# A fused attention and mixture kernel: loads written into the searched order, exponentials in place and in pairs, and a new order at the entry of the last stage

## The chip, the cores and the metric

One core of one Trainium2 chip runs the whole program. The metric is the device time of one execution in microseconds (us); lower is better. The engines are PE (TensorE; PEld are its weight loads), DVE (VectorE), ACT (ScalarE), POOL (GpSimd) and SP (SyncE, which here issues all the DMAs, strictly one after the other).

## What is computed

Three layers follow each other. Every number is float32 except w_in and w_out of the last layer, which arrive as float64 words and are turned into two narrower parts on the chip.

```python
# 1. attention with pooled keys and values: 8 batches, 8 heads, 576 queries, 72 keys of 64
k_p, v_p = k.mean over groups of 8, v.mean over groups of 8
s = q @ k_p.T / 8;  a = exp(s - max(s));  a = a / (sum(a) + 1e-9);  x = a @ v_p
# 2. soft mixture of 8 experts with 4 slots each, x is 4608 x 512
logits = x @ phi                        # 4608 x 32
d = softmax(logits over the rows);  slots = d.T @ x
out_e = relu(slots_e @ w1[e]) @ w2[e]   # w1: 512 x 1024, w2: 1024 x 512
x = softmax(logits over the slots) @ out
# 3. last layer
h = x @ w_in;  u = h * softmax(h);  ln = (u - mean(u)) / sqrt(var(u) + 1e-6) * g
y = ln @ w_out                          # 4608 x 512
```

## The kernel before

Attention works in 12 blocks n = 0..11 of 384 queries; three blocks belong to two batches b. Each block takes four pairs of heads (hp = 0..3). Its steps have short names, and one long string of names (`order`, about 730 steps) is the program order of all five engines in this stage: each engine runs its own steps in the order in which they stand there.

- On DVE: `K{b}.i` sums eight keys (L289), `M{n}.hp` takes the maxima of the scores (L371), `A{n}.hp` subtracts them into one of three spare buffers `dd_buf` (L376), `U{n}.hp` sums the exponentials (L393), `r` inverts the sums (L402), `q`, `l`, `m`, `g1`, `g2`, `gj` are small steps of the logits and the group maxima.
- On ACT: `k{b}.i` copies the summed keys (L294, L295), `E{n}.hp` takes the exponentials (L388 for hp 0, 2, 3; hp 1 is done as six short instructions straight from PSUM, L385), `t{n}.c` copies turned chunks (L419), `w`, `x`, `y` copy small products.
- On PE: `S{n}.hp` scores (L363; a float32 matmul shows as two records), `T{n}.c` transposes (L413), `P`, `X`, `Y` products of the values, `L{n}` logits (L429), `G{i}.n` the weighted sums of a group of blocks (L516).
- On POOL: `V{b}.0..2` sum eight values (L303 to L308), `R` a guard (L398), `N{n}.half` the normalisation of half a block in `a_rows` (L407). `ND` lists the halves that DVE takes in its place, here block 10, half 0.

All of attention's loads (`k0..k7`, `q0..q11`, `v0..v7`) and the first weights go through one ring buffer of 88 KB per partition: a load can be issued once the last reader of what lay there is done. They are written ahead of the order string; a planner of the framework chose where each stands in SP's queue. After them follow `D0` to `D6`: weights of the experts that are loaded into attention's own buffers when these come free (`early` holds the keys, the three spare buffers, the pooled keys and values; `a_rows` the exponentials; `late` the turned chunks). `D0` and `D1` hold the eight chunks of expert 7.

After attention, `first(e)` (L797, PE) multiplies the slots with w1 of the experts in the order 1, 2, 7, 4, 0, 5, 3, 6. Then a second hand-written list, `steps`, sets the order: `h0`, `h1` scale the hidden rows (ACT L950, DVE L952), `ph` turns them (PE L956), `B0` to `B15` multiply with w2 (PE L965), `ao2` begins the conversion of the third part of w_out (ACT L870), which is loaded into the place of `W_hi`. Behind `B15` come `a0`, `a1` (the rows of the slots copied by ACT and DVE into one tile `s2`, L1015), `s0..s3`, `so`, the conversion of the last part of w_in in halves (`aj bj sj tj +j`), `M0 M1 N0 N1` (PE L1034), `mh0 mh1` (ACT), `c0..c8` (column sums of w_out, PE L971/L972). Then the entry of the last stage: three tiles with `f` (PE L1102/L1105), `x`, `k`, `u`, `w` (DVE), `e`, `h`, `S` (ACT), `n`, `t`, `P` (PE), `T` (DVE L1162). From the seventh tile on a loop runs: per tile 24 matmuls with W_hi and W_lo (L1282, L1283, L1285), two for the next tile (L1192), and work of the other engines four tiles ahead.

Of the kernel before, what the change touches and what calls it, by code (L numbers as in the profile page):

```python
# [64 lines left out]
ND = ((10, 0),)  # L65
# [19 lines left out]
def moe_attention_kernel(ctx: ExitStack, tc, q, k, v, phi, w1, w2, w_in, w_out, g, out):  # L85
# [61 lines left out]

    for p in range(NP):
        b, n = 2 * p, NB * p
        kv_tile(kT, b, "kT")  # L150
        q_tile(n)
        if p == 0:
            for h in range(HP):
                load_kv(kT, k, b, h, h + 1)
                load_q(n, h, h + 1)
        else:
            load_kv(kT, k, b)
            load_q(n)
        for what in (LO0 if p == 0 else LO).split():
            if what == "k1":  # L160
                kv_tile(kT, b + 1, "kT")
                load_kv(kT, k, b + 1)
            elif what[0] == "v":
                kv_tile(vT, b + int(what[1]), "vT")
                load_kv(vT, v, b + int(what[1]))
            elif what == "phi":
# [66 lines left out]
    if True:  # L233
# [1212 lines left out]
```

## Time and profile before

| | us |
|---|---|
| median of three executions | 421.54 (421.21 to 423.11) |
| the profiled execution | 424.87 |
| its span, first to last instruction | 423.1 |
| PE busy in the span | 390.0 (92%) |
| DVE, ACT, POOL busy | 314.1, 295.1, 220.7 |
| read from HBM | 70.32 MB |

A "wait" in these profiles is the idle time of an engine ahead of an instruction, with what ended it in brackets. The clock column is the granted TensorE clock: 1.00 is 2.4 GHz, 0.50 is 1.2 GHz. "us to landing" of a DMA counts from its issue on SP to its completion.

### The profile page before, as it was taken

The page shows a single profiled execution, that of the slowest core. Times are in us where ns is not written, and L with a number is a line of the kernel's source. Part 1 is how long each engine was busy: PE and PEld are TensorE (multiplying, and loading weights), DVE is VectorE, ACT ScalarE, POOL GpSimd, SP SyncE. Part 2 cuts the span into 40 slices and gives each one's busy share as a digit, 9 for nine tenths or more (in the row PEclk, how much of TensorE's full clock was granted, in tenths as well). Part 3 has the DMA queues.
Part 4 walks back from the last instruction along what each step waited for, and adds up shares of the span by engine and source line. Part 5 has one row for each costly group of instructions (what it writes and reads, how often), then busy time and mean ns, then how long its engine had stood idle before and what let it go on. Part 6 is the DMA issues. An engine that isn't in the chain of part 4 may idle for free.

```text
span 423.1 us, 8679 instructions
## 1 busy us (share of the span) xinstructions
PE 390.0 (92%) x3204; PEld 235.3 (56%) x3204; DVE 314.1 (74%) x511; ACT 295.1 (70%) x663; POOL 220.7 (52%) x410
## 2 busy tenths in 40 slices
PE   4679899999989979878889989999999999999996
PEld 4568798988877435432345434444444444444445
DVE  3796999989834876894689977777777877878720
ACT  2578899899876646953469986667776666777631
POOL 4298589588540120000027687666666776666630
PEclk9996999999999997989899999999999999999999
DMA  8999999977979997994000388757666476695781
GB/s 271 389 395 417 391 419 397 362 255 270 335 277 370 400 425 310 417 419 162 0 2 1 93 167 189 161 94 169 139 135 161 89 173 156 97 174 128 141 180 50
DMA packets 86074, 97.10 MB, mean 230 GB/s; under 512 B 69904, under 2 KB 74768, under 8 KB 80144
## 3 DMA queue, kind: packets, MB, share of 16 engines
q1 hardware_dynamic: 86032, 96.55, 72.3%
q8 instruction: 25, 0.41, 0.4%
q14 instruction: 17, 0.14, 0.1%
HBM read 70.32 MB, written 9.44 MB: 189 GB/s over the span
## 4 chain that ended last, share of the span: by engine, by line
PE 52%; DMA 5%; DVE 3%; ACT 2%; issue 1%; SPq 0%; DVEq 0%; ACTq 0%
PE o L1282 14%; PE o L1283 14%; PE o L1285 13%; DMA w<-in_w_dram 4%; PE h L1192 3%; PE p L965 3%; PE pc L936 1%; DMA vhi<-v 1%; PE ph L956 1%; PE pu L1142 1%; DVE nm L1112 0%; PE o L1401 0%; PE o L1398 0%; PE h L1105 0%; PE o L1399 0%
## 5 line engine op out<-in xcount | busy, mean ns | idle before, releaser
L1282 PE MATMUL o<-W_hi,vhi 128*128 128x512 f16 x280 | 107.1, 382 | 1.6 <-DMA vhi<-v 1.6
L1283 PE MATMUL o<-W_lo,vhi 128*128 128x512 f16 x280 | 107.1, 383 | 0.0
L1285 PE MATMUL o<-W_hi,vlo 128*128 128x512 f16 x280 | 66.9, 380 | 0.0
L1204 ACT ACTIVATE e<-h,nm 128x1024 f32<-128x1024 f32 x33 | 36.7, 1113 | 43.0 <-DVE nm L1197 43.0
L363 PE MATMUL sc<-early,qT 128*128 128x144 f32 x320 | 54.4, 321 | 10.6 <-ACT early L295 9.2
L363 PEld LDWEIGHTS sc<-early,qT 128*128 128x128 f32 x320 | 47.7, 215 | 14.3 <-ACT early L295 6.0
L1263 DVE TENSOR_TENSOR v<-v,v 128x1024 f16<-128x1024 f32 x32 | 39.2, 1224 | 14.0 <-ACT v L1246 13.9
L1282 PEld LDWEIGHTS <-vhi 128*128 128x128 f16 x280 | 27.5, 98 | 35.6 <-DMA vhi<-v 2.1
L1283 PEld LDWEIGHTS <-vhi 128*128 128x128 f16 x280 | 27.6, 98 | 32.6 <-issue 0.8
L1197 DVE TENSOR_REDUCE nm<-h 128x1 f32<-128x1024 f32 x33 | 40.4, 1223 | 6.6 <-PE h L1192 6.5
L1210 DVE CUSTOM_DVE_ANT_0 u<-h,e 128x1024 f32<-128x1024 f32 x33 | 40.3, 1223 | 6.2 <-ACT e L1204 6.1
L407 POOL TENSOR_TENSOR a_rows<-a_rows,rs 128x864 f32<-128x864 f32 x23 | 37.5, 1635 | 12.1 <-DVE rs L402 4.8
L1285 PEld LDWEIGHTS <-vlo 128*128 128x128 f16 x280 | 25.1, 98 | 33.6 <-issue 7.8
L1246 ACT ACTIVATE v<-u,b,sr 128x1024 f32<-128x1024 f32 x33 | 40.8, 1236 | 1.5 <-POOL b L1234 1.5
L1221 ACT ACTIVATE e<-u,nmu 128x1024 f32<-128x1024 f32 x33 | 37.9, 1149 | 0.4 <-POOL nmu L1216 0.4
L371 DVE TENSOR_REDUCE nmax<-sc 128x6 f32<-128x432 f32 x48 | 28.3, 597 | 9.9 <-PE sc L363 9.7
L1259 DVE TENSOR_SCALAR v<-u,nmu,sr 128x1024 f16<-128x1024 f32 x32 | 26.0, 811 | 10.2 <-POOL sr L1232 10.2
L413 PE MATMUL pt<-ident,a_rows 128*128 128x128 f32 x180 | 28.3, 284 | 3.8 <-ACT late L419 2.3
L1228 POOL TENSOR_TENSOR y<-y 128x1 f32<-128x1 f32 x33 | 30.3, 918 | 2.7
L1232 POOL TENSOR_TENSOR sr<-z,exponents 128x3 f32<-128x3 f32 x33 | 29.2, 883 | 2.7
L419 ACT ACTIVATE late<-pt 128x384 f32<-128x384 f32 x60 | 27.7, 490 | 4.1 <-PE pt L413 3.4
L1295 ACT ACTIVATE ob<-o,r 128x512 f32<-128x512 f32 x32 | 21.7, 679 | 9.7 <-PE o L1285 9.7
(246 smaller groups left out, 741.0 us busy)
## 6 DMA issues: line engine op xcount, KB each, us to landing
w<-in_w_dram SPq DMA_DIRECT2D x16, 1024.0 KB, 10.9
vT<-in_v_dram SPq DMA_DIRECT2D x8, 1152.0 KB, 12.4
out_dram<-ob SPq DMA_DIRECT2D x11, 768.0 KB, 3.6
kT<-in_k_dram SPq DMA_DIRECT2D x7, 1152.0 KB, 12.0
w<-in_w_dram SPq DMA_DIRECT2D x12, 512.0 KB, 4.8
qT<-in_q_dram SPq DMA_DIRECT2D x7, 768.0 KB, 12.9
a_rows<-in_w_dram SPq DMA_DIRECT2D x4, 1024.0 KB, 9.0
qT<-in_q_dram SPq DMA_DIRECT2D x8, 384.0 KB, 10.9
```

Of the source, the lines that this page charges most:

```text
L363: pe.matmul(sc[:, r].rearrange("p h j -> p (h j)"), qT[n][:, hp, x, :], BD[b % NBD][:, hp, :], start=(i == 0), stop=(i == len(hv) - 1))
L407: eng.tensor_tensor(av, av, st["rs", n, hf].unsqueeze(3).to_broadcast([P, NR, 4, J]), ALU.mult)
L1197: dve.tensor_reduce(nm, ft[i][0], axis=AX.X, op=ALU.max, negate=True)
L1204: act.activation(e, hv, AF.Exp, bias=nm, accum_out=st[:, 0:1])
L1210: dve.tensor_tensor_reduce(u, hv, e, 1.0, 0.0, ALU.mult, ALU.add, st[:, 1:2])
L1221: act.activation(e, u, AF.Square, bias=nmu, accum_out=st[:, 2:3])
L1228: pool.tensor_tensor(y, y, y, ALU.mult)
L1246: act.activation(v, u, AF.Identity, bias=b, scale=sr[:, 0:1])
L1263: dve.tensor_tensor(v2, u_t[i]["v"], u_t[i]["v1"], ALU.subtract)
L1282: pe.matmul(po, hi[:, c, :], W_hi[:, c, :], start=(c == 0), stop=False)
L1283: pe.matmul(po, hi[:, c, :], W_lo[:, c, :], start=False, stop=False)
L1285: pe.matmul(po, lo[:, c, :], W_hi[:, c, :], start=False, stop=(c == NFC - 1))
```

## The change

1. The loads of attention after the first pair of batches, and the first weights, are steps of the order string now (`ik3`, `iq4`, `iv2`, `ia1.2`, `io0`, `ir4`, `ib0.1`): SP issues them in the written order. Keys go ahead of queries; w_out's first two parts (`io0`, `io1`), which stood between `q5` and `v3`, go far back.
2. `A` writes into the place of the exponentials in `a_rows`, `E` works in place, and heads 2 and 3 of a block are one instruction of `E` and of `U`. The three spare buffers fall away, and three of expert 7's eight chunks (`ir7`) are loaded into their place in the midst of attention; `D1` shrinks from four chunks to one.
3. Sixteen matmuls of the identity with itself (`F0` to `F15`) are added to PE's queue; their result is not used.
4. DVE no longer takes a normalisation (`ND` is empty).
5. The order of attention is a new one.
6. `s2` becomes two tiles, `a1` no longer follows `a0`, `so` moves from DVE to ACT; `c1` to `c7` move ahead of `B13` to `B15`; `G8` and `g8` move behind the conversion; six unused matmuls of 512 columns are added (`y0`, `y1`); the entry of the last stage has a new order.

```diff
-ND = ((10, 0),)
+ND = ()
...
-        dd_buf = [early[:, 1152 + 512 * i:1664 + 512 * i] for i in range(3)]
-        kp_buf, vp_buf = (early[:, x:x + 576].rearrange("p (b h j) -> p b h j", b=2, h=HP) for x in (2688, 3264))
-        WT_buf = early[:, 3840:4416]
+        kp_buf, vp_buf = (early[:, x:x + 576].rearrange("p (b h j) -> p b h j", b=2, h=HP) for x in (1152, 1728))
+        WT_buf = early[:, 2304:2880]
+        loads["ir7"] = beside, (7, 5, early, 2880, 3)
...
-            dd = st["dd", n, hp] = dd_buf[st.get("dd", 0)][:, 0:NR * 2 * J].rearrange("p (r h j) -> p r h j", r=NR, h=2)
-            st["dd"] = (st.get("dd", 0) + 1) % 3
-            dve.tensor_tensor(dd, st["sc", n, hp], st["nmax", n, hp].unsqueeze(3).to_broadcast([P, NR, 2, J]), ALU.add)
+            ah = a_buf[n % NA][:, :, 2 * J * hp:2 * J * hp + 2 * J].rearrange("p r (h j) -> p r h j", h=2)
+            dve.tensor_tensor(ah, st["sc", n, hp], st["nmax", n, hp].unsqueeze(3).to_broadcast([P, NR, 2, J]), ALU.add)
...
+                w = pair(n, hp)
+                ah = a[:, :, 2 * J * hp:2 * J * (hp + w)]
+                act.activation(ah, ah, AF.Exp)
+        def pair(n, hp):
+            return 2 if hp % 2 == 0 and not on_act(n, hp) and not on_act(n, hp + 1) else 1
...
+        def busy(i):
+            if i == 0:
+                st["busy"] = misc("busy", [P, P], "gg")
+            pe.matmul(st["busy"], ident, ident, start=True, stop=True)
...
         def sums_done():
-            beside(7, 4, early, 2048, 4)
+            beside(7, 4, early, 2048, 1)
...
-        order = ("K0.0 K0.1 K0.2 k0.0 k0.1 k0.2 S0.0 S0.1 S0.2 M0.0 M0.1 M0.2 A0.0 A0.2 K0.3 E0.0 k0.3 E0.1 S0.3 U0.0 K1.0 Z0 Z1 Z2 R0.0 B1 r0.0 "
-                 "M0.3 A0.3 K1.1 E0.2 k1.0 E0.3 k1.1 S1.0 S1.1 S1.2 N0.0 M1.0 A1.0 M1.1 U0.2 M1.2 A1.2 U0.3 E1.0 E1.1 S1.3 V0.0 V0.1 V0.2 R0.1 M1.3 "
...
+        order = ("K0.0 K0.1 K0.2 k0.0 k0.1 k0.2 S0.0 S0.1 S0.2 M0.0 A0.0 M0.1 M0.2 K0.3 E0.0 E0.1 k0.3 S0.3 F0 F1 F2 F3 F4 F5 F6 F7 F8 U0.0 A0.2 "
+                 "M0.3 A0.3 K1.0 K1.1 E0.2 k1.0 k1.1 Z0 B1 R0.0 F9 F10 F11 S1.0 S1.1 S1.2 U0.2 r0.0 M1.0 A1.0 M1.1 N0.0 R0.1 E1.0 E1.1 S1.3 r0.1 "
+                 "M1.2 M1.3 U1.0 A1.2 A1.3 N0.1 R1.0 T0.0 T0.1 S2.0 S2.1 S2.2 t0.0 t0.1 E1.2 ik2 iq3 ik3 r1.0 M2.0 A2.0 M2.1 U1.2 M2.2 K2.0 V0.0 "
+                 "V0.1 V0.2 N1.0 R1.1 T0.2 T0.3 F12 F13 F14 P0 S2.3 E2.0 E2.1 t0.2 w0.1 w0.0 w0.2 w0.3 t0.3 k2.0 U2.0 M2.3 A2.2 r1.1 A2.3 K2.1 T0.4 "
+                 "X0 S3.0 S3.1 R2.0 N1.1 V1.0 x0.1 t0.4 x0.0 E2.2 k2.1 M3.0 r2.0 A3.0 U2.2 M3.1 Y0 L0 T1.0 T1.1 S3.2 S3.3 y0 E3.0 t1.0 t1.1 E3.1 iq4 "
+                 "iv2 ik4 iq5 iv3 iq6 R2.1 V1.1 V1.2 B4 m0 M3.2 K3.0 U3.0 r2.1 A3.2 M3.3 A3.3 l0 K3.1 T1.2 T1.3 F15 P1 k3.0 t1.2 t1.3 w1.3 w1.2 w1.0 "
...
+                 "x2.0 E5.0 t3.0 E5.1 gd0 t3.1 T3.2 Y2 S5.3 Q2 gb0 ia2.2 iv4 ia2.3 ik5 iq7 ik6 iq9 iv5 iq8 U5.0 A5.2 g10 q2 g20 gj0 r4.1 M5.3 A5.3 "
...
+                 "P5 ia1.2 ik7 iq10 iv7 ir7 io0 ir4 iv6 iq11 K7.1 M9.0 M9.1 A9.0 l6 U8.2 K7.0 V7.0 R8.1 B10 t7.1 t7.2 E9.0 k7.1 E9.1 k7.0 w5.2 w5.0 "
...
+                 "q11 gj4 g24 lm gE4 lf la0 la1 G4.11 ia6.0 ia6.1 ib1.0 ia1.3 ia2.1 ia1.1 io1 ia1.0 ib0.0 ia6.3 ib0.1 ia2.0 ib1.1 D2 ia6.2 D0 D3 D5 "
+                 "D4 D1 D6 e0 e1 e2 la2 lt0 es lt1 lT0 lT1 ld0 ld1 lT2 ls0 ls1 lz lo0 cs lo1 ge4").split()
...
-                 'g6 c0 B12 +i1 bi2 c1 si2 G6 g7 B13 ti2 B14 c2 p8 B15 +i2 g8 G7 a0 c3 aj0 a1 G8 bj0 aj1 s0 s1 s2 s3 c4 sj0 so bj1 '
-                 'tj0 M0 +j0 M1 N0 sj1 tj1 +j1 c5 N1 c6 mh0 c7 mh1 c8 X '
-                 'f00 f01 n0 S0 x00 x01 k0 n1 e00 e01 S1 T0 u00 f10 t00 u01 h00 t01 h01 T1 P0a w00 x10 m0 f11 w01 x11 k1 e10 e11 P0al '
...
+                 'H4 H5 G2 W4 W5 H1 g5 p4 H7 H6 g4 H0 H2 B10 W3 W1 W6 ai1 G5 G4 B11 W2 bi1 W0 W7 si1 ai2 p6 p7 ti1 g6 c0 c1 B12 c2 c3 +i1 '
+                 'bi2 si2 G6 g7 B13 c4 c5 ti2 B14 c6 c7 p8 B15 +i2 G7 a0 a1 s0 s1 s2 aj0 bj0 s3 so aj1 bj1 sj0 M0 tj0 +j0 sj1 tj1 +j1 g8 '
+                 'N0 mh0 M1 N1 mh1 G8 c8 X f00 x00 f01 x01 k0 e00 u00 n0 S0 T0 e01 u01 n1 y0 S1 T1 t00 h00 w00 f10 y1 t01 h01 P0a f11 w01 '
...
+    def busy(n):
+        for c in range(n):
+            pe.matmul(pu0[:, 1].rearrange("p c d -> p (c d)"), ones_h, W_hi[:, c, :], start=True, stop=True)
...
+    op("y0", "n1", busy, 4)
+    op("y1", "f10", busy, 2)
```

## Rows read from the trace of the kernel before

**Rows 1.** Stretches of 10 us: busy PE, PEld, DVE, ACT, POOL; clock, DMA share, GB/s.

```profile
30.00:40.00 10.00, 7.66 (x52) 6.89 (x51) 6.62 (x12) 8.28 (x34) 8.53 (x9) 0.66 1.02 418
...
50.00:60.00 10.00, 10.00 (x133) 9.33 (x133) 9.29 (x22) 9.35 (x40) 6.44 (x6) 1.00 1.04 406
...
220.00:230.00 10.00, 10.00 (x50) 5.17 (x49) 9.78 (x17) 9.77 (x18) 6.44 (x27) 1.00 0.00 1
...
250.00:260.00 10.00, 10.00 (x48) 4.59 (x46) 6.45 (x7) 6.35 (x10) 7.39 (x15) 1.00 0.90 190
```

**Rows 2.** PE in order of time, first 50 us: start, length, line, records.

```profile
5.24 3.67 PE L363 MATMUL sc<-early,qT 128*128 128x144 f32 x12 [5.24 <-ACT early L295]
...
13.84 2.29 PE L363 MATMUL sc<-early,qT 128*128 128x144 f32 x8 [2.95 <-ACT early L295]
16.95 6.36 PE L363 MATMUL sc<-early,qT 128*128 128x144 f32 x30 [0.82 <-POOL qT L348]
...
32.50 0.90 PE L413 MATMUL pt<-ident,a_rows 128*128 128x128 f32 x3 [2.34 <-ACT late L419]
...
38.35 1.82 PE L363 MATMUL sc<-early,qT 128*128 128x144 f32 x12
...
40.75 1.29 PE L429 MATMUL plt<-late,W 128*32 128x128 f32 x30
```

**Rows 3.** Groups by line over the whole span: busy, mean ns of one, idle before.

```profile
L1197 DVE TENSOR_REDUCE nm<-h 128x1 f32<-128x1024 f32 x33 | 40.4, 1223 | 6.6 <-PE h L1192 6.5
...
L1204 ACT ACTIVATE e<-h,nm 128x1024 f32<-128x1024 f32 x33 | 36.7, 1113 | 43.0 <-DVE nm L1197 43.0
...
L393 DVE TENSOR_REDUCE ssum<-a_rows 128x6 f32<-128x432 f32 x36 | 20.4, 591 | 2.5 <-ACT a_rows L385 2.4 <-POOL a_rows L407 0.2
L388 ACT ACTIVATE a_rows<-early 128x432 f32<-128x432 f32 x36 | 20.1, 564 | 6.6 <-DVE early L376 5.7 <-DVE ssum L393 0.2
```

**Rows 4.** SP's queue in order of time: start, length, line.

```profile
79.50 0.33 SPq L132 DMA_DIRECT2D kT<-in_k_dram  x1
...
122.44 2.00 SPq L202 DMA_DIRECT2D a_rows<-in_w_dram  x3
...
144.41 0.33 SPq L195 DMA_DIRECT2D W_hi<-in_w_out_dram  x1
...
165.25 1.19 SPq L182 DMA_DIRECT2D w<-in_w_dram  x2
```

**Rows 5.** ACT in order of time, behind the last expert of w1.

```profile
156.43 1.12 ACT L870 ACTIVATE cv_y<-W_hi 128x1024 f32<-128x1024 f32 x1 [5.37 <-DMA W_hi<-in_w_out_dram]
157.44 0.69 ACT L950 ACTIVATE h<-p,zr 128x512 f32<-128x512 f32 x1
```

**Rows 6.** DVE in order of time: one hidden half, then from the last w2 matmul on.

```profile
154.92 0.75 DVE L952 TENSOR_SCALAR h<-p,zr 128x512 f32<-128x512 f32 x1 [1.12 <-PE p L797]
...
195.77 0.74 DVE L946 SCALAR_TENSOR_TENSOR cS<-cS,lo_rows,pc 128x512 fp32r<-128x512 f32 x1
...
199.66 0.69 DVE L887 CUSTOM_DVE_ANT_0 win<-raw,cv_y 128x1024 uint16<-128x1024 uint16 x1
203.32 0.69 DVE L1112 TENSOR_REDUCE nm<-h 128x1 f32<-128x512 f32 x1 [2.97 <-PE h L1105]
...
209.94 0.69 DVE L1151 TENSOR_TENSOR vlo<-pu,vhi 128x512 f16<-128x512 f32 x1 [1.33 <-ACT vhi L1148]
...
212.95 0.69 DVE L1112 TENSOR_REDUCE nm<-h 128x1 f32<-128x512 f32 x1 [1.13 <-PE h L1102]
```

**Rows 7.** PE in order of time: the hidden rows turned, then the entry of the last stage.

```profile
158.18 2.13 PE L956 MATMUL ph<-sel,h 128*128 128x32 f32 x9 [2.43 <-ACT h L950]
...
202.26 1.88 PE L1105 MATMUL h<-hTm,c_first 128*128 128x512 f32 x4
...
209.42 0.63 PE L1283 MATMUL o<-W_lo,vhi 128*128 128x512 f16 x1
...
211.98 0.63 PE L1283 MATMUL o<-W_lo,vhi 128*128 128x512 f16 x1
```

More of the change, by code (lines that the diff above doesn't have):

```diff
@@ L57 @@
 WL = 0
+NF = 16
 NPRE = 8
@@ L146, in load_q, with load_in @@
             sp.dma_start(qT[n][:, h0:h1], q[n].rearrange("p (h r t) -> p h r t", h=HP, r=NR)[:, h0:h1])
+    loads = {}
+    def load_in(what, i):
+        if what == "q":
+            load_q(i)
+        else:
+            load_kv(*((kT, k) if what == "k" else (vT, v)), i)
     for p in range(NP):
@@ L156, in moe_attention_kernel, with load_part, load_w @@
         else:
-            load_kv(kT, k, b)
-            load_q(n)
+            loads[f"ik{b}"] = load_in, ("k", b)
+            loads[f"iq{n}"] = load_in, ("q", n)
         for what in (LO0 if p == 0 else LO).split():
[L160 to L166, printed above, removed]
+            if what == "phi":
                 for h2 in range(2):
                     sp.dma_start(phi_z[64 * h2:64 * h2 + 64, :, h2, :], phi[64 * h2:64 * h2 + 64])
-            elif what == "g":
+                continue
+            if what == "g":
                 sp.dma_start(g_sb, g)
-            else:
-                q_tile(n + int(what[1]))
-                load_q(n + int(what[1]))
+                continue
+            i = (n if what[0] == "q" else b) + int(what[1])
+            if what[0] == "q":
+                q_tile(i)
+            else:
+                kv_tile(kT if what[0] == "k" else vT, i, what[0] + "T")
+            if p == 0:
+                load_in(what[0], i)
+            else:
+                loads["i" + what[0] + str(i)] = load_in, (what[0], i)
     w1t, wo_raw, w2t, wi_raw, win = {}, {}, {}, {}, {}
-    def load_w(store, src, e, name):
+    def load_part(t, src, e, i, n):
+        sp.dma_start(t.rearrange("p k f -> p (k f)"), src[e, i // 4, :, 512 * (i % 4):512 * (i % 4 + n)])
+    def load_w(store, src, e, name, later=None):
         n = WQ if store is w1t else WQ2
@@ L181, in load_w @@
             t = ring.tile([P, n, 512], F32, name=f"{name}_{e}{i}")
-            sp.dma_start(t.rearrange("p k f -> p (k f)"), src[e, i // 4, :, 512 * (i % 4):512 * (i % 4 + n)])
+            if later:
+                loads[f"{later}{e}.{i // n}"] = load_part, (t, src, e, i, n)
+            else:
+                load_part(t, src, e, i, n)
             for j in range(n):
@@ L205, in beside @@
             i, n, c0 = i + m, n - m, c0 + 512 * m
-    def load_rest(e, i):
-        t = ring.tile([P, 8 - i, 512], F32, name=f"w1_{e}r").rearrange("p k f -> p (k f)")
-        beside(e, i, t, 0, 8 - i)
     def load_next(what):
@@ L225, in load_next, with first_raw @@
                 win[kk] = ring.tile([P, DF], F32, name=f"win{kk}")
+    def first_raw(i):
+        load_raw(wo_raw, w_out, i, "wo_raw")
     for x in SEQ[:NPRE]:
-        load_next(x)
+        kind, i = x[0], int(x[1])
+        if kind == "a":
+            load_w(w1t, w1, i, "w1", "ia")
+        elif kind == "b":
+            load_w(w2t, w2, i, "w2", "ib")
+        elif kind == "o":
+            loads[f"io{i}"] = first_raw, (i,)
+        else:
+            t = ring.tile([P, 8 - REST[i], 512], F32, name=f"w1_{i}r").rearrange("p k f -> p (k f)")
+            loads[f"ir{i}"] = beside, (i, REST[i], t, 0, 8 - REST[i])
     psE = None
@@ L387, in exps @@
             else:
-                act.activation(a[:, :, 2 * J * hp:2 * J * hp + 2 * J], st["dd", n, hp].rearrange("p r h j -> p r (h j)"), AF.Exp)
+                w = pair(n, hp)
[3 more added lines that the diff above has]
+            return 2 if hp % 2 == 0 and not on_act(n, hp) and not on_act(n, hp + 1) else 1
         def sums(n, hp):
-            ah = a_buf[n % NA][:, :, 2 * J * hp:2 * J * hp + 2 * J].rearrange("p r (h j) -> p r h j", h=2)
-            x = 2 * (hp % 2)
-            dve.tensor_reduce(st["sum", n][:, hp // 2, :, x:x + 2], ah, axis=AX.X, op=ALU.add)
+            w, x = 2 * pair(n, hp), 2 * (hp % 2)
+            ah = a_buf[n % NA][:, :, 2 * J * hp:2 * J * hp + J * w].rearrange("p r (h j) -> p r h j", h=w)
+            dve.tensor_reduce(st["sum", n][:, hp // 2, :, x:x + w], ah, axis=AX.X, op=ALU.add)
         def sums_guard(n, hf):
@@ L683, in last_group @@
             beside(3, 4, a_rows[1], 3072, 4)
-        steps = {}
+        steps = dict(loads)
         def step(name, f, *args):
             steps[name] = f, args
+        for i in range(NF):
+            step(f"F{i}", busy, i)
         for b in range(2 * NP):
@@ L712, in moe_attention_kernel @@
                 step(f"M{n}.{i}", scores_max, n, i)
+                second = i % 2 and pair(n, i - 1) == 2
                 if not on_act(n, i):
                     step(f"A{n}.{i}", scores_less, n, i)
-                    step(f"U{n}.{i}", sums, n, i)
-                step(f"E{n}.{i}", exps, n, i)
+                    if not second:
+                        step(f"U{n}.{i}", sums, n, i)
+                if not second:
+                    step(f"E{n}.{i}", exps, n, i)
             for i in range(2):
@@ L817, in moe_attention_kernel @@
     hTm = pers.tile([P, NFC, NE * 36], F32, name="hTm")
-    s2 = pers.tile([P, 512], F32, name="s2")
+    s2 = [pers.tile([P, 256], F32, name=f"s2{i}") for i in range(2)]
     so = pers.tile([P, HP, S], F32, name="so")
@@ L1011, in slot_rows @@
         def slot_rows(x):
-            if x == 0:
+            if "ps" not in t1:
                 t1["ps"] = psE.tile([P, HP, S], F32, name="ps", tag="ph")
-            d, p = s2[:, 256 * x:256 * x + 256], p2[:, 256 * x:256 * x + 256]
+            d, p = s2[x], p2[:, 256 * x:256 * x + 256]
             act.activation(d, p, AF.Copy) if x == 0 else dve.tensor_copy(d, p)
         def slot_sums(kk):
-            pe.matmul(t1["ps"][:, kk, :], s2[:, P * kk:P * kk + P], sel4[:, 0:S], start=True, stop=True)
+            pe.matmul(t1["ps"][:, kk, :], s2[kk // 2][:, P * (kk % 2):P * (kk % 2) + P], sel4[:, 0:S], start=True, stop=True)
         def slots_out():
-            dve.tensor_copy(so, t1["ps"])
+            act.activation(so, t1["ps"], AF.Copy)
         def last_exponent(hf):
@@ L1040, in moe_attention_kernel @@
         op("a0", f"B{2 * NE - 1}", slot_rows, 0)
-        op("a1", f"a0 B{2 * NE - 1}", slot_rows, 1)
+        op("a1", f"B{2 * NE - 1}", slot_rows, 1)
         for kk in range(HP):
@@ L1054, in moe_attention_kernel @@
             op(f"mh{hf}", f"N{hf}", m_high, hf)
-        steps = ('ao1 ao0 x1 x2 so0 so1 bo0 to0 bo1 to1 x3 +o1 q2 +o0 A6 q0 x4 hm x5 x6 q3 q1 ao2 h1 so2 h0 p0 ph p1 g0 bo2 to2 hT '
[9 rows of a table removed]
-                 'Gy6 R4 Fe9 Ga7 P5a Ff9 P5bl Gc7 Ff8 R5 Gx7 Fg8 Fg9 Ga8 Gb8 Gy7 Gx8 Gc8 Gy8 K1').split()
+        steps = ('ao1 ao0 x1 x2 so0 so1 bo0 to0 bo1 to1 x3 +o1 q2 +o0 A6 q0 x4 hm x5 x6 q3 q1 ao2 h1 so2 h0 p0 ph p1 g0 bo2 to2 hT B0 +o2 '
[8 rows of a table added]
+                 'Gc6 Gx5 Fc9 Gb7 Gy5 Fd9 Ga7 Gx6 Gy6 Gx7 Fg8 Gb8 P5a P5bl R5 Fe9 Ff9 Gx8 Ga8 Gc7 Gy7 Fg9 Gc8 Gy8 K1').split()
         assert sorted(set(steps)) == sorted(steps)
@@ L1323, in moe_attention_kernel @@
             op(f"u{i}{hf}", f"e{i}{hf} k{i}", raw_u, i, hf)
-            op(f"t{i}{hf}", f"u{i}{hf}" + (f" t{i}0" if hf else ""), raw_turn, i, hf)
+            op(f"t{i}{hf}", f"u{i}{hf}" + (f" t{i}0" if hf else "") + (" y0 y1" if hf and not i else ""), raw_turn, i, hf)
             op(f"h{i}{hf}", f"t{i}{hf}", raw_hi, i, hf)
```

3 lines of the change are left out of this document (removed), and 53 rows, old and new, of tables (order, steps).

## The prediction, made before the changed kernel was run

> **What bounds the kernel now.** I read the table of stretches first [rows 1]. The reader is to see three regimes. From 250 us to the end PE never waits; the loop there is untouched, so the change can only move the moment at which it begins. From 50 to 110 us PE is again busy all the time (six stretches, the first is shown), with DVE near 9 of 10: attention's middle is bound by PE, and relief for DVE and ACT is worth little there. Ahead of that, PE loses time in two ways, which PE's own timeline shows [rows 2]: it waits (2.95, 0.82, 2.34 us), and it runs at half rate. A record of the scores takes 3.67/12 = 0.306 us at the start and 1.82/12 = 0.152 us at 38 us, so the clock was at 1.2 GHz early on, and again around 35 us, where its mean is 0.66 over ten microseconds [rows 1]. Then comes a stage held by loads: all 70.3 MB must be in before the last stage, DMA moves some 0.405 MB per us when full [rows 1], and SP's queue stands on buffers that are not free [rows 4]. The last weights wait for the first w2 product at 165.25, which waits for the hidden rows at 157.44, which stand in ACT's queue behind a conversion that waited 5.37 us for a load [rows 5]. Last, the entry of the final stage: DVE idles 2.97, 1.33 and 1.13 us, and a W_lo record takes 0.63 us at half clock [rows 6, 7].
>
> **The change part by part.** All terms are against the profiled execution: 424.87 us, 3.33 over the median 421.54. What they sum to is taken off the median as well.
>
> *Start of attention.* Before, `S1.0` begins at 16.95 and `L0` ends at 40.75 + 1.29 = 42.04 [rows 2]. In the new order `K0.3` stands ahead of `A0.2`, but `k0.3` behind `E0.1` (six short instructions); I get `S0.3` at 12.9 to 14.7 in place of 13.84. Then come twelve `F` in one piece. `F` is two records of 128 columns, by the scores' two rates 0.27 us at full clock and 0.54 us at half. I let six run at half rate (3.3 us) and six at full (1.6), so `S1.0` starts at 19.7, 2.8 later than now; its keys (`M0.3 A0.3 K1.0 K1.1` on DVE, then ACT) are ready at about 18, so the `F` are not all hidden. From there to the end of `L0` PE has 80 score records (12.2 us at 0.152), 21 transposes (0.82 us for six, 2.9), `L0` 1.29, and some 2.3 of small products and three more `F`: 18.7 us at full clock. Of the waits I leave 1.3 us (`P0` behind `V0`, which moves behind `N0.1` on POOL; `S3.0` behind `k2.0`). 19.7 + 18.7 + 1.3 = 39.7: 2.3 us earlier. Ends: clock up at once and no wait left, 2.7 us better, -5; clock no sooner than now, all `F` at half rate (+1.6) and the old waits of 2.3 us more, +1.5. I take -2.2, as the two rates are measured and only the moment of the rise is not.
>
> *Middle of attention.* Twelve `E` and twelve `U` go. From 564 ns at 432 columns and 1113 at 1024 [rows 3] the fixed part of an `E` is 0.16 us, of a `U` (591, 1223) 0.13: ACT loses 2.0 us, DVE 1.6 and the normalisation of (10, 0). POOL gets that one; behind it in POOL's queue stand `N10.1` and `V7`, and `T10` waits for them. `A` now must wait until `G` and `T` of six blocks before have read `a_rows`: `A6.0` for `G0.0`, `A9.0` for `G1.3`, both on PE just ahead; behind `A9.0` on DVE stand `U8.2`, `K7.0`, and PE's next scores wait for a free bank. I price it at 0 to 1 us each. As PE is full there, I count 0 for all of this, ends -1 and +2.
>
> *Loads.* `io0` and `io1` (2.1 MB) leave the early queue, where no load was late anyway. `k7` needs the place of `q7`, free after `S7.3`; now it is issued at 79.50 as the last one [rows 4], and in the new order `q10`, `v7`, `v6`, `q11` stand behind it. So SP stands there with nothing to move, and 45.6 MB are left where 39.7 were. From `k7` to W_hi's part of w_out are 29.7 MB, 73.3 us. `S7.3` moves ahead of `L4` and three `T5` (2.7 us) and is 2.2 us earlier, so `k7` goes at 74.6, with 2 us until bytes flow; a hole of 4 us before `D2` (its release is at 122.44 now [rows 4]). That gives 154 for W_hi in place of 156.4 [rows 5]: -2.4. So the loads just follow attention, and I let `B0` and all after it move by -2.2. What hides a wait here is that `e` 1 and 2 are multiplied while `D1` is on its way: `D1` stands behind `D4` now and lands at 144 by the same sum, while PE wants it at 141: 2.9 us of wait. Most of it lies under W_hi's: `h1` is ready to run at 154.92 now [rows 6] and `h0` only at 157.44, 2.5 us later. The rest I leave to the later waits for loads, which then fall away. Ends: -4 and +2.
>
> Here a rule of the Trainium skill speaks against the change: DMA: Bandwidth & Descriptors, "Anatomy of one DMA", says that a semaphore wait happens on the issuing sequencer before dispatch and the DMA engines only consume their queues. By that rule one load that waits keeps all later ones off the engines, and a fixed order can lose what the planner won. SP's timeline agrees: the queue stands before `k7` until 79.50 [rows 4].
>
> *From `B15` to the last stage.* After `B15` DVE's chain is `a1` (behind `a0`), `G8` 0.74, `so`, then the conversion, whose last step starts at 199.66 [rows 6]. `G8` and `so` leave DVE's path and `a1` runs beside `a0`; but its input is the last load (about 196), and `c6 c7` delay `B15` by 0.4. The conversion ends 0.3 to 0.7 us earlier. `c6 c7` (four records, 0.9 us at half of 0.43 each) no longer stand between `N1` and `f00` on PE, `f00` starts before `mh1`. Together `x01` starts 1.3 us earlier: `c` is free where it goes, as PE waits for w2 there; without that cover it would cost 3.5. Ends 0 and -2.2.
>
> *Entry of the last stage.* `y0`, `y1` are six such records of 0.22 us, where PE waits for `T0` and `u` (0.6 to 0.7 us each time), so 1.3 us cost nothing or 0.6. They and the earlier `f` are to keep the clock at 2.4 GHz: the eight records with W_hi and W_lo from 209.1 on begin (211.98 - 209.42)/6 = 0.43 us apart [rows 7], at the full rate it would be half, 1.7 us less. In the new order `u00` goes ahead of `T0`, and `f11` comes some 2 us sooner after `f00`. But DVE and ACT are at 9.8 of 10 from 220 to 230 [rows 1], so what counts is DVE's idle time, 5.4 us in the three waits [rows 6], of which 1.3 were counted above; of the rest I take half, -2.1. Ends 0 and -4.
>
> Sum: -2.2 + 0 - 1.3 - 2.1 = -5.6, so 424.87 would become 419.3, and the median 421.54 becomes 415.9.
>
> **Rivals.** (1) The loads hold: `k7` and `D2` leave holes, W_hi lands at 156 as before, and the start's gain is lost; -1.3 - 2.1 = -3.4, 418.1. For it: the standing queue [rows 4]; against it: no loads are late in attention now, and `ir7` fills a hole. (2) More: the start gives -5; the wait of 2.43 us ahead of the hidden rows goes and with it the half clock, at which nine records take 2.13 us, sixteen 3.8 [rows 7], -1.9; the ways into and through the entry give -1.3 and -2.8: -11, 410.5. (3) It doesn't do what it says: the `F` cost what they give, the entry is held by DVE and ACT: -0.5, 421.0. (4) Slower, by one mechanism: PE stops for `D1`, and the clock falls to 1.2 GHz as it did after the waits ahead of 35 and of 158 us. The first of those falls lasted 6.8 us (a mean of 0.66 over ten [rows 1]); at half rate the w1 products then lose 3.4. With the start at its bad end, `h1` runs at 154.92 + 1.5 + 2.9 + 3.4 = 162.7, `h0` beside it, 5.3 later than 157.44; with 1.3 and 2.1 gained behind it that is +1.9, with half of those gains +3.6: 425.1. It decides once `D1` lands over 2.5 us after PE wants it and attention is not earlier; against it stands that the sum above has attention 2.2 us earlier.
>
> One more rule: TensorE: Matmul & The Clock Gate, "What's actually happening", says that throttled is the default state. The clock column reads 1.00 up to 21 us; taken at its word the `F` would cost 3.3 us, not 4.9, and `S1.0` start at 18. The lengths of the scores [rows 2] speak for the skill, so I do not take that.
>
> **How the numbers follow.** Forecast 0.50, rival (1) 0.15, (2) 0.15, (3) 0.12, (4) 0.08. A measurement of this kernel tells about 0.5% (2.1 us) from no change. Faster: 0.50 + 0.15 + 0.15 = 0.80; same 0.12; slower 0.08. The range of 410.5 to 421.0 takes in the forecast with its ends and rivals (1) and (2), and leaves out the slower case and about half of (3).
>
> **What the profile after would show.** Right: the clock at 1.00 through 30 to 40 us and through the entry; `L0` ended near 40; `S1.0` near 20; W_hi's conversion waiting until about 154; a wait of PE for `early` in the w1 products of up to 3 us; `x01` near 200.5; the loop unchanged at 250 us and later, only shifted. Wrong: holes in DMA of over 8 us between 45 and 125 us, then attention's end matters less than W_hi's landing (rival 1); a PE clock of 0.5 in 140 to 150 us (rival 4); DVE waits in front of `A6` or `A9` over 1 us each.

## The result, and the profile after

After takes 416.95 us (median of eight executions, 416.36 to 419.29), before 422.84 (median of eight, 419.40 to 425.07). The ratio is 0.988, with an interval of 0.985 to 0.991, that is 5.1 us less, 3.8 to 6.3; the two medians lie 5.9 apart. The forecast was 5.6 less.

The two profiled executions lie further apart, 424.87 and 417.35 (spans 423.1 and 415.5): that of before was 2.0 above its median of eight, that of after 0.4. Cut at marks that both traces have, the 7.6 us of span lie here (a load lands at its issue plus its time to landing; PE's marks are the starts of records):

| stretch | before | after | difference |
|---|---|---|---|
| start to the first score | 5.24 | 5.18 | -0.06 |
| to the score record a third of the way (107th of 320) | 39.79 | 34.57 | -5.22 |
| to the first w1 product | 93.91 | 91.22 | -2.69 |
| to the landing of W_hi's part of w_out | 17.46 | 20.39 | +2.93 |
| to `B0`, the first w2 product | 7.04 | 4.64 | -2.40 |
| to the landing of the last load | 32.90 | 33.14 | +0.24 |
| to `f00` | 5.92 | 4.87 | -1.05 |
| to the first product with W_hi | 6.85 | 8.91 | +2.06 |
| to the end of the span | 213.99 | 212.58 | -1.41 |

The table of stretches, first of before and then of after, cut at the third of the scores and the first w1 product (columns as in [rows 1]):

```profile
5.24:45.03 39.79, 31.73 (x218) 27.32 (x219) 30.12 (x53) 25.21 (x96) 24.97 (x30) 0.91 1.02 397
45.03:138.94 93.91, 91.19 (x1390) 80.21 (x1388) 73.53 (x188) 80.41 (x275) 56.48 (x56) 1.00 0.90 340
```

```profile
5.18:39.75 34.57, 28.51 (x239) 26.16 (x240) 29.79 (x50) 23.54 (x88) 20.23 (x25) 0.95 1.03 395
39.75:130.97 91.22, 90.58 (x1399) 81.27 (x1397) 72.79 (x177) 79.80 (x270) 63.51 (x64) 1.00 0.93 359
```

In the first part PE is idle 6.06 us instead of 8.06 and busy 3.22 less, although the `F` are in it: fewer records run at half rate. About 1 us of the 5.22 is only moved: ten records of small products (into `pW`, `pv` and `pl`) stand ahead of the mark in the old order and behind it in the new one. In the second part PE is idle 0.64 instead of 2.72.

PE of after in order of time, which answers to [rows 2] and [rows 7]: the start, then the w1 products, the hidden rows and w2, then the entry of the last stage.

```profile
12.67 1.00 PE L386 MATMUL sc<-early,qT 128*128 128x144 f32 x6 [1.92 <-ACT early L318]
13.51 4.47 PE L694 MATMUL busy<-ident 128*128 128x128 f32 x24
17.82 4.09 PE L386 MATMUL sc<-early,qT 128*128 128x144 f32 x32
21.74 0.27 PE L441 MATMUL pt<-ident,a_rows 128*128 128x128 f32 x1
...
33.12 1.29 PE L457 MATMUL plt<-late,W 128*32 128x128 f32 x30
...
134.43 1.11 PE L837 MATMUL p<-early,slotm 128*32 128x512 f32 x8
140.56 1.94 PE L837 MATMUL p<-early,slotm 128*32 128x512 f32 x8 [5.02 <-DMA early<-in_w_dram]
...
153.20 1.97 PE L996 MATMUL ph<-sel,h 128*128 128x32 f32 x16 [0.51 <-ACT h L990]
155.10 1.08 PE L976 MATMUL pc<-ident,L_all 128*32 128x128 f32 x32
156.00 6.19 PE L1005 MATMUL p<-w,hTm 128*32 128x512 f32 x56
...
194.01 1.99 PE L1144 MATMUL h<-hTm,c_first 128*128 128x512 f32 x4
...
201.54 0.73 PE L1205 MATMUL pu<-W_hi,ones_h 128*128 128x512 f16 x2 [1.74 <-DVE vlo L1190]
202.06 1.06 PE L1181 MATMUL pu<-ident,u 128*128 128x128 f32 x4
202.92 0.63 PE L1325 MATMUL o<-W_hi,vhi 128*128 128x512 f16 x1
```

The reader is to see the `F` (L694), whose 24 records take 4.47 us (they start 0.11 us apart up to 14.2 us and 0.21 apart up to 17.4, so at both rates), the wait of 5.02 us for `D1`, the hidden rows (L996) at full rate where [rows 7] had them at half, and half rate again at 202.92.

ACT of after behind the last expert of w1, as [rows 5], and DVE in the entry, as [rows 6]:

```profile
151.38 1.19 ACT L910 ACTIVATE cv_y<-W_hi 128x1024 f32<-128x1024 f32 x1 [3.65 <-DMA W_hi<-in_w_out_dram]
152.47 0.67 ACT L990 ACTIVATE h<-p,zr 128x512 f32<-128x512 f32 x1
```

```profile
195.17 0.69 DVE L1151 TENSOR_REDUCE nm<-h 128x1 f32<-128x512 f32 x1 [1.53 <-PE h L1144]
...
203.79 0.69 DVE L1190 TENSOR_TENSOR vlo<-pu,vhi 128x512 f16<-128x512 f32 x1 [2.30 <-ACT vhi L1187]
206.25 1.29 DVE L1151 TENSOR_REDUCE nm<-h 128x1 f32<-128x512 f32 x2 [1.77 <-PE h L1141]
```

The conversion still stands ahead of the hidden rows and still waits for its load, until 151.4 instead of 156.4. In the entry DVE's three longest waits are 5.60 us together, where [rows 6] has 5.43.

Groups of after over the whole span, as [rows 3]: a pair costs 926 ns on ACT and 1041 on DVE, two single ones 2 x 562 and 2 x 591; twelve of each saved 2.4 and 1.7 us of work (forecast 2.0 and 1.6).

```profile
L421 DVE TENSOR_REDUCE ssum<-a_rows 128x12 f32<-128x864 f32 x12 | 12.5, 1041 | 0.8 <-ACT a_rows L412 0.8
L412 ACT ACTIVATE a_rows<-a_rows 128x864 f32<-128x864 f32 x12 | 11.1, 926 | 3.1 <-DVE a_rows L398 2.9
```

### The profile page after: what moved, and what is told of

It reads as the page before. It is cut to its first block, busy times and chain, and to the rows that moved or that the text cites. A ratio compares the mean times of both kernels' runs of the same rounds, so it can differ in the third digit from the quotient of the medians.

```text
span 415.5 us, 8701 instructions
## 1 busy us (share of the span) xinstructions
PE 383.4 (92%) x3242; PEld 231.8 (56%) x3242; DVE 309.1 (74%) x496; ACT 293.2 (71%) x652; POOL 222.2 (53%) x412
## 4 chain that ended last, share of the span: by engine, by line
PE 76%; DMA 11%; DVE 5%; ACT 4%; issue 1%; POOL 1%; SPq 0%; DVEq 0%; ACTq 0%; POOLq 0%
PE o L1325 14%; PE o L1326 14%; PE o L1328 13%; PE sc L386 9%; PE pt L441 5%; PE plt L457 4%; PE h L1235 3%; DMA w<-in_w_dram 3%; DMA W_lo<-in_w_out_dram 3%; DMA early<-in_w_dram 3%; PE pG L544 2%; PE p L837 1%; DMA kT<-in_k_dram 1%; DMA vhi<-v 1%; PE busy L694 1%
## 5 line engine op out<-in xcount | busy, mean ns | idle before, releaser
L386 PE MATMUL sc<-early,qT 128*128 128x144 f32 x320 | 46.3, 298 | 8.2 <-ACT early L318 8.2
L386 PEld LDWEIGHTS sc<-early,qT 128*128 128x128 f32 x320 | 42.6, 198 | 9.5 <-POOL sel L289 5.1
L435 POOL TENSOR_TENSOR a_rows<-a_rows,rs 128x864 f32<-128x864 f32 x24 | 39.2, 1632 | 11.5 <-DVE rs L430 9.8
L1271 POOL TENSOR_TENSOR y<-y 128x1 f32<-128x1 f32 x33 | 29.2, 885 | 2.7
## 6 DMA issues: line engine op xcount, KB each, us to landing
qT<-in_q_dram SPq DMA_DIRECT2D x7, 768.0 KB, 12.7
```

The lines of the kernel that those rows point to most:

```text
L386: pe.matmul(sc[:, r].rearrange("p h j -> p (h j)"), qT[n][:, hp, x, :], BD[b % NBD][:, hp, :], start=(i == 0), stop=(i == len(hv) - 1))
L435: eng.tensor_tensor(av, av, st["rs", n, hf].unsqueeze(3).to_broadcast([P, NR, 4, J]), ALU.mult)
```

## The experiments

All are timed in five rounds beside before; their ratios to before stand beside 0.988 for after.

**The F.** One kernel is after without them, the other is before with them alone.

```diff
-NF = 16
+NF = 0
...
+        order = [x for x in order if x[0] != "F"]
```

> The kernel after without the sixteen F; all else as after (416.95 us). Theory (the F pay through the clock): the profile after shows half clock only from 14 to 18 us and full clock from 18 us on, where before had a second stretch near 35 us; without the F, S1.0 starts near 15 instead of 17.8, but a stretch of half clock of some 5 us comes back between 20 and 45 us, and the score records are 2 to 4 us late from 40 us on: 419 to 421 us. Rival (the new order alone took away the stops of PE, the F cost what they give): S1.0 near 15, no second stretch of half clock, 415 to 417 us.

```diff
+NF = 16
...
+        for i, ahead in zip(range(NF), ["U0.0"] * 9 + ["S1.0"] * 3 + ["P0"] * 3 + ["P1"]):
+            order.insert(order.index(ahead), f"F{i}")
```

> The kernel before with the sixteen F alone, at the places that they have after (nine behind S0.3, three ahead of S1.0, three ahead of P0, one ahead of P1). Theory from the run without F (the order takes the second stretch of half clock away, the F only the first, which is worth some 1.5 us): the stretch near 31 to 38 us stays, as the waits of PE ahead of it stay; 421 to 422.5 us against 422.4. Rival (the F pay in any order, by keeping the clock up): no half clock near 35 us and 417.5 to 419.5 us.

Without the `F`: 418.46 us, ratio 0.990 (0.986 to 0.994). Before with them: 423.03 us, 1.001 (0.998 to 1.004). PE without the `F`, and PE and the stretch of 30 to 40 us of before with them:

```profile
17.79 5.79 PE L386 MATMUL sc<-early,qT 128*128 128x144 f32 x28 [2.33 <-ACT early L318]
```

```profile
33.65 0.90 PE L414 MATMUL pt<-ident,a_rows 128*128 128x128 f32 x3 [2.24 <-ACT late L420]
...
35.84 3.09 PE L364 MATMUL sc<-early,qT 128*128 128x144 f32 x12
```

```profile
30.00:40.00 10.00, 7.74 (x53) 6.97 (x52) 6.82 (x12) 8.12 (x30) 8.00 (x9) 0.66 1.01 418
```

Without them the second stretch of half clock does not come back (the clock reads 1.00 from 30 to 40 us), and in the old order they do not remove it, as the waits that precede it are still there. So it was not the `F` that took it away but the rest of the change to attention; the order, the exponentials in place and the loads were not tried one by one. My expectation for the first kernel fell in its reason, and 418.46 lies between its two ranges. What the `F` buy is full rate sooner: the scores start 0.12 us apart from 17.5 us on in after, and from 22.1 us on without the `F`, where `L0` ends at 36.1 instead of 34.4. Whether that is worth anything at the end stays open: 1.5 us between the medians, but the intervals overlap.

**The pairs.**

```diff
-            return 2 if hp % 2 == 0 and not on_act(n, hp) and not on_act(n, hp + 1) else 1
+            return 1
...
+        order = [y for x in order for y in ((x, x[:-1] + "3") if x[0] in "EU" and x[-2:] == ".2" else (x,))]
```

> The kernel after with every E and U as two instructions again (the second right behind the first); in-place exponentials, order and loads as after (416.95 us). The prediction's step: ACT loses 2.0 us of work by the pairs and DVE 1.6, and it counts 0 of that on the path as PE is full between 50 and 120 us: 416.3 to 417.8 us. Rival (from the profile after, where attention gains another 3 us between 40 and 90 us and DVE is 9.7 of 10 busy there): the pairs carry that gain, the twelfths of the scores from 50 us on are 2 to 3 us later and the time is 419 to 420 us.

418.36 us, ratio 0.990 (0.985 to 0.995). From the third of the scores to the first w1 product it takes 93.5 us; the kernels with the pairs and the same attention as after take 91.2 to 95.0. By neither measure is it told apart from after: 0 to 1.4 us.

**The loads.** First `io0` and `io1` back between `iq5` and `iv3`, then loads moved so that they fill the gaps in the DMA.

```diff
+        def put(what, ahead):
+            order.remove(what)
+            order.insert(order.index(ahead), what)
+        put("io0", "iv3")
+        put("io1", "iv3")
```

> The kernel after with io0 and io1 (2.1 MB, about 5 us of the engines of DMA) back where before had them, between iq5 and iv3. Theory (DMA stands still near 44 us and near 92 us because places are not free, not because there are no free loads): io0 and io1 fill the gap at 43 to 47 us, v3, q6 land 5 us later (46 and 51 instead of 44 and 46), attention is not later by more than 1 us, and the bytes left behind 92 us are 2.5 us fewer: 414 to 417 us. Rival (the prediction's: the early queue is better without them, attention waits for v3 and q6): attention ends 2 to 4 us later, 418 to 421 us.

```diff
...
+        put("io0", "ia2.2")
+        put("ir7", "ik7")
+        put("ia1.1", "ia6.0")
+        put("ia1.0", "ia6.0")
+        put("ia2.1", "ia6.0")
+        put("ia1.3", "ia6.0")
+        put("ia2.0", "ia6.0")
+        put("D1", "D5")
```

> The kernel after with loads moved in SP's order only: io0 ahead of ia2.2, ir7 ahead of ik7, the five parts ia1.1 ia1.0 ia2.1 ia1.3 ia2.0 ahead of ia6.0, D1 ahead of D5. Theory (all loads behind 93 us run without a gap, so the gaps at 43 to 47, at 70 to 72 and at 91 to 93.5 us, some 6 us together, set when the last load lands): the gaps fill by 4 us or more, the last load lands at 185 to 186 instead of 189.1 and the time falls by 3 to 4 us, 413 to 414 us. Rival (places that become free late, and the conversions on DVE and ACT, set the pace of the loads behind 112 us): new gaps open near 112, 126 and 157 us, and the time stays at 416 to 417 us.

`io0` and `io1` in the early queue: 416.99 us, ratio 0.986 (0.982 to 0.991), the same as after. The filled gaps: 419.15 us, 0.992 (0.989 to 0.995), 2.2 us above after by the medians, with intervals that overlap at their ends. Two stretches of after, then of the filled kernel:

```profile
92.00:94.00 2.00, 2.00 (x18) 1.81 (x17) 1.84 (x4) 1.84 (x7) 1.92 (x2) 1.00 0.27 77
112.00:114.00 2.00, 2.00 (x44) 1.44 (x40) 1.36 (x5) 1.88 (x5) 0.32 (x1) 1.00 1.00 412
```

```profile
92.00:94.00 2.00, 2.00 (x19) 1.81 (x18) 1.84 (x4) 1.88 (x6) 1.92 (x2) 1.00 1.04 395
112.00:114.00 2.00, 2.00 (x38) 1.69 (x36) 1.95 (x5) 1.88 (x6) 1.10 (x2) 1.00 0.04 16
```

The gap at 92 to 94 us is full (DMA share 1.04 instead of 0.27), and another one is open at 112 to 114: SP now stands there for a place that POOL's sum of the values frees. W_hi's part lands at 151.24 instead of 151.36. So with the earlier gaps filled, the places that attention frees hold the loads at 112 us: in this the rival was right. In after itself the DMA has no gap there; it is full from 94 us on until W_hi has landed. That the kernel is no faster than after has another cause, which the next three kernels show, as they move `D1` too.

**D1, and where PE stops.** `D1` ahead of `D5` alone; the same with 22 unused matmuls ahead of the hidden rows' turn; the same with the hidden rows ahead of the conversion.

```diff
...
+        put("D1", "D5")
```

> The kernel after with D1 ahead of D5 and D4. PE's wait of 5.02 us for D1 in the w1 products goes (D1 lands near 133 instead of 140.5), and with it the half clock behind it at 141 to 144 us. Theory (the end of the loads, not PE, sets the last stage): the hidden rows still wait for the conversion of W_hi, the last load still lands near 189 us, the time stays at 416.3 to 417.5 us. Rival (the prediction's mechanism against the change, rival 4, at its full price): the wait and the half clock cost 3 to 5 us on the path, 412 to 414 us.

```diff
...
+        def busy_hidden(n):
+            for _ in range(n):
+                pe.matmul(ph_all[:, NFC:NFC + 4, :].rearrange("p c s -> p (c s)"), ident, ident, start=True, stop=True)
...
+        op("yh", "", busy_hidden, 22)
...
-        steps = ('... h1 so2 h0 p0 ph p1 ...
+        steps = ('... h1 so2 h0 p0 yh ph p1 ...
```

> The kernel with D1 ahead of D5 (420.07 us), and 22 unused matmuls of 128 columns (44 records, some 4.8 us) between the last w1 product and the turned hidden rows, where PE stood 5.55 us. Theory (what D1 ahead of D5 cost is the clock alone: it moved PE's stop from 135 us, where the half clock was over before the hidden rows came, to just ahead of them): the sixteen ph records take 2 us instead of 3.6, B0 to B6 6.2 instead of 7.9, B0's place is free 2.5 us earlier and the time is 416.5 to 418 us. Rival (it is the order of the loads, not the clock): 419 to 421 us.

```diff
-        steps = ('... q3 q1 ao2 h1 so2 h0 p0 ph p1 g0 bo2 to2 hT B0 +o2 '
+        steps = ('... q3 q1 h1 h0 p0 ph p1 g0 hT ao2 so2 bo2 to2 B0 +o2 '
```

> The kernel with D1 ahead of D5, and the conversion of the third part of w_out (ao2 so2 bo2 to2) behind the hidden rows (h1 h0 p0 ph p1 g0 hT) instead of ahead of them. Theory: the hidden rows run right behind the last w1 product, 4 to 5 us earlier against the landing of W_hi, PE doesn't stop there and the clock stays up; the places of B0 to B3 are free earlier, the stream of loads, which is full anyway, has no gap near 160 us: 416 to 417.5 us. Rival (the conversion that is now late holds the loads of w_in behind it): a gap in the loads near 160 to 170 us and 418 to 420 us.

`D1` early alone: 420.07 us, ratio 0.995 (0.992 to 0.998), some 3 us slower than after. With the unused matmuls: 417.27 us, 0.990 (0.986 to 0.993). With the hidden rows first: 417.53 us, 0.990 (0.987 to 0.993). PE with `D1` early:

```profile
156.47 3.62 PE L1000 MATMUL ph<-sel,h 128*128 128x32 f32 x16 [5.55 <-ACT h L994]
160.02 1.94 PE L980 MATMUL pc<-ident,L_all 128*32 128x128 f32 x32
161.73 7.93 PE L1009 MATMUL p<-w,hTm 128*32 128x512 f32 x56
```

The same with the unused matmuls (L1005, 37 of their 44 records):

```profile
147.78 4.29 PE L1005 MATMUL ph<-ident 128*128 128x128 f32 x37
152.53 1.97 PE L1001 MATMUL ph<-sel,h 128*128 128x32 f32 x16 [0.45 <-ACT h L995]
154.43 1.08 PE L981 MATMUL pc<-ident,L_all 128*32 128x128 f32 x32
155.33 6.19 PE L1014 MATMUL p<-w,hTm 128*32 128x512 f32 x56
```

The DMA behind the start of `B0`, with `D1` early (`B0` at 161.73) and in after (at 156.00); the last three columns are clock, DMA share and GB/s:

```profile
162.00:164.00 2.00, 2.00 (x12) 0.40 (x8) 1.35 (x2) 1.98 (x4) 0.00 (x0) 0.50 0.32 127
164.00:166.00 2.00, 2.00 (x16) 0.49 (x12) 1.62 (x3) 2.00 (x3) 0.00 (x0) 0.69 0.60 147
```

```profile
156.00:158.00 2.00, 2.00 (x28) 0.65 (x24) 1.21 (x3) 1.30 (x3) 0.00 (x0) 1.00 1.01 418
158.00:160.00 2.00, 2.00 (x24) 0.65 (x20) 0.28 (x1) 1.14 (x2) 0.00 (x0) 1.00 1.01 381
```

So my expectation for the first of the three was wrong, and the next two show why. In the order of after the hidden rows wait for W_hi's load wherever `D1` stands. With `D1` early PE finishes w1 sooner and stops right ahead of the hidden rows; they, and the first products of w2, then run at 1.2 GHz, `B0`'s place is free later, and the DMA has a gap. With `D1` late PE stops at 135.5 us, half rate falls on w1 products that have time, and PE is at 2.4 GHz from 144 us on when the hidden rows come. Work that keeps PE busy, or an order in which it need not wait, brings back 2.8 and 2.5 us.

The traces show the same where attention does not enter: from W_hi's landing to that of the last load it is 41.2 us with `D1` early, 37.8 in after, 39.1 with the unused matmuls, 38.3 with the hidden rows first, and 39.9 in before, which has the stop, the half rate and the gap too (a DMA share of 0.19 at 164 to 166 us). This guards against a flaw of the trace with `D1` early: its execution took 422.61 us, 2.5 above the median, and PE also stood 1.85 us at 119 us in it. The filled kernel, which has `D1` early as well, has no such stop at 119 us and shows the same wait (5.56 us) and the same 3.62 us for the hidden rows. Nor is the early stop always free: in all six traces with `D1` late the hidden rows take 1.97 us, but in three of them half rate lasted 6.8 us, w1 ended too late, and `B0` came 5.0 to 6.0 us behind W_hi's landing instead of 4.6.

**The ramp.** After without `y0` and `y1`; before with part 6 of the change alone; before with parts 1 to 5 alone.

```diff
-    op("y0", "n1", busy, 4)
-    op("y1", "f10", busy, 2)
...
```

> The kernel after without y0 and y1; all else as after (416.95 us). Theory (they do not pay): after still shows half clock from 202.9 to 205 us and PE waits 1.74 us for DVE behind y0, so the entry is held by DVE and the time stays within 0.7 us: 416.3 to 417.7. Rival (they keep the clock up where it would have fallen earlier): the half-clock stretch in the entry becomes longer by 2 to 4 us and the time is 418 to 419 us.

> The kernel before with part 6 of the change alone (two tiles s2, so on ACT, the order of the steps from B12 on, y0 and y1). Prediction's terms: -1.3 on the way to the last stage and -2.1 in its entry, 3.4 us below before, about 419.4. Theory from the two profiles: from the landing of the last load to the end of the span it is 226.8 us before and 226.4 after, so part 6 gives 0.4 us and no more: 422 to 422.8 us against 422.84.

> The kernel before with parts 1 to 5 alone (attention and its loads; the steps behind it as before). Prediction's terms: 2.2 us below before, about 420.6. Theory from the two profiles: the last load lands 7.2 us earlier after than before, and all of that comes from attention and the loads, so this kernel has nearly the whole gain: 416.5 to 418 us.

Without `y`: 417.58 us, ratio 0.988 (0.985 to 0.992), the same. The ramp alone: 422.53 us, 1.001 (0.998 to 1.004), nothing. Attention and loads alone: 418.62 us, 0.991 (0.988 to 0.994), most of the gain; what after has beyond it lies inside the intervals. The entry in all traces, from the start of `f00` to the end of the span, sorted by the granted clock there:

| entry | clock 1.00 throughout | a stretch at 0.50 |
|---|---|---|
| old order | 219.6, 219.6 | 220.8 (before) |
| new order | 219.8, 219.9, 219.9, 220.0, 220.3 | 221.5 (after), 221.5, 221.7, 221.8 |
| new order without `y` | 219.5, 219.7 | |

At equal clock the new entry is no shorter than the old one, and with the `y` in it the clock fell in four traces of nine. Only the way into it is shorter: from the last load's landing to `f00` it is 5.91 or 5.92 us in every trace with the old steps and 4.9 or less with the new.

**What the pieces give together.** The filled gaps, the hidden rows ahead of the conversion, and no `y` (the diffs above).

> The kernel with the filled gaps (io0, ir7, five parts of w1 and D1 moved; 419.15 us), the hidden rows ahead of the conversion of the third part of w_out, and without y0 and y1. Theory: what the filled gaps bring (2 us at 113 us) was lost to the half clock ahead of the hidden rows and to the gap in the loads behind it; without these the last load lands near 187 us: 413.5 to 416 us. Rival (the places that attention frees late set the loads' pace whatever stands in front): the last load lands at 189 as after, 416 to 417.5 us.

415.54 us (414.26 to 416.90), ratio 0.984 (0.981 to 0.987): 1.4 us below after by the medians, the best of all, though its interval overlaps that of after. The last load lands at 188.2, not at 187; half of what was expected came. It also tells what the filled gaps are worth: 2.0 us against the kernel with the hidden rows first, which lacks them (and still has the `y`, worth nothing above); with `D1` early alone as the base it was 0.9. Both point the same way, but the intervals touch or overlap.

## Why the prediction was right, step by step

The sum was right, -5.6 against -5.1 (-3.8 to -6.3), but by terms that missed in both directions; that it came so close is luck.

**Start of attention: right in sign, too small.** -2.2 was taken, with an end of -5; -5.2 was measured to the third of the scores, and -3.7 to -5.5 in the other kernels with after's attention. About 1 us of it is work moved behind the mark. Two terms were mis-sized. I counted 80 score records up to `L0`; the new order has 68 (32, 18, 6 and 12 in PE's rows). And I divided the length of a row by its count, 1.82/12 = 0.152 us: the last record's overlap with the next is in that length. From 17.82 to 21.74 thirty-two records take 3.92 us, 0.122 each. 80 x 0.152 = 12.2 us should have been 68 x 0.122 = 8.3. The Trainium skill (Perfetto Trace Analysis, "Tensor Engine Instruction (MATMUL, LD_WEIGHTS)") states that the profiled end of a matmul is estimated, not observed. These rows agree. `L0`'s end, forecast for 39.7 and found at 34.4, was also no like-for-like mark, as `S3.2`, `S3.3`, `T1.0`, `T1.1` and `P1`, which stood ahead of it, now follow it. Nearly right was `S0.3` (12.7, forecast 12.9 to 14.7). Right was that the `F` would not all be hidden, but `S1.0` starts at 17.8, 0.9 us later than before, where 19.7, 2.8 later, was forecast. Without the `F` four of its eight records run from 14.3 us on, and the other four wait for their keys until 17.8 as well.

**Middle of attention: 0 was taken, -2.7 measured in this pair, -1.4 in the median of the eight other kernels with its order and pairs.** The reading "PE is full" came from the stretch of 50 to 110 us alone. Half of PE's idle 2.72 us in this part of before lay behind 110 us, outside what I read, and after has 0.64 in all. Which part of the change removed it was not tried. DVE had no wait ahead of `A6` or `A9` over 1 us, as forecast.

**Loads: half right.** "The loads just follow attention" held for 5.0 of 8.0 us. `k7` went at 71.1 (forecast 74.6), W_hi landed at 151.4 (154), `D1` at 140.5 (144). The missing 2.9 us are rival (1) in part: there are holes, but not where it put them all. Behind 2 us the DMA share in after is under 0.85 at 42 to 48, 70 to 72 (ahead of `k7`) and 90 to 94 us; ahead of `D2`, where I counted a hole, it is full. When the holes are filled, the places freed at 112 us hold the loads back in their turn. The rule cited in the prediction (the Trainium skill, DMA: Bandwidth & Descriptors, "Anatomy of one DMA") shows at 92 to 94 us: SP stood before one load with five behind it that could have gone, and the DMA share was 0.27. Filling the gaps did not make W_hi land sooner (151.24 against 151.36, in a trace whose attention ended 0.9 us later), and 0.9 to 2.0 us came of it at the end, not told from nothing.

**D1 and the hidden rows: the mechanism was found, with the wrong sign.** I forecast a wait for `D1` of up to 3 us that costs nothing and, as rival (4), one that makes the clock fall and costs up to 5.3. It was 5.0 us, the clock fell (0.61 and 0.54 at 140 to 144 us, which I had named as a sign of being wrong), and it pays: with `D1` early instead, the time is 3 us more. The gain of 2.4 us between W_hi's landing and `B0` is what rival (2) called "the half clock goes", -1.9; I had given that a chance of 0.15 and left it out of the forecast.

**From `B15` to the last stage: right**, -1.3 against -1.05 (at least that in every trace with the new steps).

**Entry: wrong.** -2.1 was taken, 0 is shown at equal clock, +0.65 in this pair. "Of the rest I take half" had no row behind it. Rival (3) had it: DVE and ACT hold the entry, and DVE's waits there are as long as before. The clock did not stay up through the entry either.

In this pair start, middle and hidden rows gave 8.2 us more than forecast, loads, way and entry 6.2 less; the pair itself lies 1.6 us further apart than the medians.

## What to carry to other kernels

When an engine must wait for a load anyway, ask where it will stand idle: a stop far ahead of the critical product leaves time for the clock to come back, the same stop right ahead of it cost 3 us here, and removing an early wait can bring on the late one. A gap in the loads that is filled can open again where the next place becomes free late; look for that release before moving anything. And time a pipelined engine by the distance of starts, over a counted number of records, not by a row's length.

## What the runs showed of the hardware that was not expected

Executions of one kernel differ by 3 to 6 us (2.9 among the eight of after, 5.7 among those of before). In some traces PE stands still with nothing to wait for that the profile shows, in three of them ahead of the same transpose. PE of after without `y`, whose attention is that of after, and its DMA queues from 113 to 116 us:

```profile
117.54 0.88 PE L441 MATMUL pt<-ident,a_rows 128*128 128x128 f32 x6 [1.29 <-issue]
```

```profile
q8 instruction: 1, 0.02, 2.1%
```

In the profile of after there is no such wait, and the packet of instructions of that time was moved between 110 and 113 us; with attention alone changed it came at 116.6, and PE stood 1.57 us at 119. The DMA was full from 112 to 118 us in all three (shares of 0.98 to 1.06). The other traces fit in part: with `D1` early the packet came at 116.7 and PE stood 1.85 us; in four more it came at 110.4 to 112.2 and PE did not stop; but with `io0` and `io1` early it came at 114.5, without the `F` one came at 116.4, and PE did not stop either. That late packets of instructions cause these stops is a guess that was not tried.

The clock column does not show the state ahead of its first change: in after it reads 1.00 up to 14 us, but the scores from 7.5 us on start 0.24 us apart, where 0.122 is the full rate.
